# An attention and feed-forward kernel on one core: a new order of the same operations, and row factors of unit 0 spread by two TensorE products

## Chip, cores and metric

One core of a Trainium2 chip runs the whole program in one launch. The metric is the device time of that launch in microseconds (us); a kernel's time is the median of its runs. Engines are named as the profile names them: PE is TensorE's matrix multiply and PEld its weight load, DVE is VectorE, ACT ScalarE, POOL GpSimd, SP SyncE, which issues the DMAs.

## What is computed

Attention in which a query sees only the keys of its own hash bucket (six sign bits of a projection), for 4 batches of 8 heads with 768 tokens of 64 values, and behind it a feed-forward layer with the Mish function for the 3072 tokens. The two weight matrices arrive as 64-bit floats.

```python
q_bits = (np.einsum('bhsd,dk->bhsk', q, proj) > 0)        # k_bits likewise, 6 bits
mask = q_bucket[:, :, :, None] == k_bucket[:, :, None, :]
scores = np.where(mask, scale * np.matmul(q, k.transpose(0, 1, 3, 2)), -1e9)
attn = np.exp(scores - np.max(scores, axis=-1, keepdims=True))
attn = attn / (np.sum(attn, axis=-1, keepdims=True) + 1e-09)
x = np.matmul(attn, v)                                    # to 3072 x 512
h = x @ w_in                                              # 512 x 2048
out = (h * np.tanh(np.log1p(np.exp(h)))) @ w_out          # 2048 x 512
```

## The kernel before

The work is cut into 12 units (4 batches, 3 pairs of 128-row chunks). A unit has 8 **scores** n (4 pairs of heads, 2 chunks), 96 in all, and behind them 8 groups of the feed-forward layer, which run about three blocks of four scores later. For each score:

- `S` on PE (line 879): eight products of queries (`QT`) and keys (`KT`) into `ps_s`, 128 x 1536 in PSUM, two heads beside each other. From unit 1 on there is one `ps_s`, so the next score's products wait until this score's exponentials have read it.
- `max` on DVE (line 885) over `ps_s`, then `scl` (lines 891 to 897), two to four tiny instructions on DVE or POOL that make the scale and bias of the exponential. They come as two instructions on 128x2 or, with the same result, four on 128x1.
- `exp` on ACT (line 910), once per head, from `ps_s` into one of three buffers `pb`, with row sums. Where ACT ran Mish last, a table load stands before it.
- `sums` (lines 923, 926) and `rv`, the reciprocal (line 939, DVE): the row factors.
- `hi` for each head (lines 373, 375, 376 for POOL, ACT, DVE): `pb` times the row factor, as 16-bit floats, into `hl`; then `lo`, what `hi` left over. On DVE `lo` is one instruction with two SBUF inputs (line 391); on POOL it is two (line 397 scales `pb` in place, line 398 subtracts `hl`). Only after `lo` is that `pb` buffer free.
- a DMA transposes `hl` into `PT` (line 408), and `V` on PE (line 997) multiplies `PT` by the values.

Keys, queries, values and weights are split into a high and a low 16-bit part in the same manner (`k_lo`, `q_lo`, `v_lo`, `w_lo`, all through lines 391 or 397/398); the first 24 scores run beside the conversion of the weights from 64-bit floats (lines 540 to 565). The feed-forward group is `H` (lines 1053 to 1055) into `ps_acc`, Mish on ACT (line 1071), `g_hi` and `g_lo` (lines 373 to 376, 391) into `ffb`, and `O` (lines 1104 to 1106).

Unit 0 differs: its exponentials are transposed on PE as 32-bit floats, and the row factors are applied after `V`. `rvw` (line 935, DVE) writes the reciprocals spread over 128 columns into a piece of `X`; `rvb` (line 943, PE) multiplies that by a unit matrix (`ffb` holds it) into `ps_g`; `rvc` copies it out.

Nothing is scheduled while the kernel runs. `Plan.op` records every operation with its alternatives, `alts` (which engine does it, and in which form), and `ORDER`, a string of 2753 numbers, gives the sequence: the number names the operation, a letter b, c or d behind it the second, third or fourth alternative. Each engine runs its instructions in that sequence.

Of the kernel before, what the change touches and what calls it, by code (L numbers as in the profile page):

```python
# [18 lines left out]
P = 128  # L19
# [68 lines left out]
1 88 0 5 2 3 4 14 22 23 24 25b 38b 13 40 6 37 7 8 9 10 11b 63 73 39c 65 78 18 19 20 21 53c 55b 26c 41 42 27 74 75 76  # L88
15 67 43 72 54c 66 44 307 12 45 46 83 47 48 49 104 28b 29 79 62 168 30b 31 77b 89 91b 32 34 213 214 215 90c 50 51 64
33 80 84 52 35 81 82 92 105 85 86 87 107 113 216b 114c 115c 116b 106 36 108 109 56 57 58 59 60 110 68 217 71 17 93 94  # L90
95 96 97 99 98 16 100 61 117 169 170 171 172 173c 175 176 256 372 153c 112 101 102 103b 257 258 111 129 130 132 133
134 152 154b 155 156 70 135 136 137 138 139 118 119 120 121 122 147 148 131 123b 124b 125 157 158 205 206b 140b 69 162
163b 164 144 149 150 151 182c 177 159 160 161 178 308 309 310b 145 146b 373 374 183 126 185 186 187 141 188 189 190
142 458 200 211 218b 191 192 459 197 198 201 202 203 174c 460 461b 193b 378 379 204 219c 194 128 143b 195 184 196 127
230 222 223 224 180 179 181 199b 225 243 212 462 380 165 166 226 227 207b 208 254 228 229 240 241 464 167 244 245b 210
209 220 221 255 231b 232 233 234 465 466 311 242 268 248c 249b 236b 237 259 246 269 270 250 251 235 286 247 273c 274
238 265 266 293c 239 262c 263 305 312b 306 252 267 287 272 271 279 381 253 294b 280 283 284 275b 276 278 299 288 289
277 295c 296 300b 298 297 301 264 285 281 292 291 290 313b 314 315b 370 282 371 326c 327 317b 318 321 322 323 324 432
434 302 303 304 332 333 334 328c 329 331 330 325 352 353 433 457 344d 456 316 319b 345 347b 350b 260c 335 336 354 435
# [12 lines left out]
679 699 680b 681 720 746 718 683b 725c 726 721c 672 754 673 727 612 722 768 799 690 691 692c 694 695 767 747 751 755
693c 696 697 752b 753 613 748b 749 806 757b 758b 728 729 730 731 759 760 761 763 856 807 808 809 769 684 682b 733 734
775 735 736 762 770 771 772 764 798 685 774 800 737 686 687 860 773 801 857 873 688 756 689 738 765b 855 739 740 741
861 877 790d 791 793c 796 797 802 803 792c 794 864 862b 863 742 743 744 874 804 805 821 858 859 895 766 812 813 814c
816b 795 810b 815b 875c 822 776 777 778 779 780 811b 910 820 881 823 781c 783 818 876 878 879 824 825 847d 848 849 880
745 851 931 782b 868 869 882 961 700 894 817 850b 865 870 784 785 786 909 788 826 827 828 829 830 831 872 883 871 896
911 945 819 852 853b 854 932 832b 886 887 889 787 888c 962 897 917 898b 890b 900 842 899 789 912 833 835 891 834b 836
892 893 933 934 964 901b 902 903b 913 914b 915 905 906 843 844 845 1147 916 937c 965 968 969 938 918 904b 907b 939c
941 942 908 948 949 837 838 977 978 981 846 963 970c 950 951 940b 943b 944 979c 980 966c 967 1046 952 972 840 953 954  # L120
956b 959b 982 983 971 1047 839 955c 919 935b 920 921 922b 924b 1050 1051 946 957 985 958 960 973 1148 925 866 974 976
975 988 1064 989 991c 990 992b 998 999 1000b 994 1020 1001 1060 1021 1022 841 923c 1002 1003c 1004 1005b 984 1061 997
993 1006c 1007b 1102 926 927 1054 884 885b 1014 867 1149 1015 995 1009 1010 1008 996 1011 1048b 1049 1065 1013 928
# [115 lines left out]
def lsh_attention_mish_ffn(  # L239
# [10 lines left out]
    nc = tc.nc  # L250
    B, H, S, D = q.shape
# [17 lines left out]
    op = plan.op  # L269
# [14 lines left out]
    unit = ffb.rearrange("p n e -> p (n e)")[:, 3584:3712]  # L284
    UNIT = ("ff", 3584, 3712)
# [134 lines left out]
    def dve(name, ns, fn, reads, writes, frees=None):  # L420
        return op(name, [("DVE", ns, fn)], reads, writes, frees=frees)
# [838 lines left out]
```

## Time and profile before

| what | us |
|---|---|
| median of 3 runs | 964.82 (963.01 to 965.0) |
| the profiled execution's own time | 964.74 |
| its span, first to last instruction | 963.0 |
| PE, DVE, ACT, POOL busy | 831.7, 733.8, 574.2, 513.3 |
| mean granted TensorE clock | 0.957 of full |

Outside the span lie 1.74 us. A busy time is the union of an engine's instructions and includes what an instruction spends blocked after it has started.

### The profile page before, as it was taken

How to read it: one execution, taken by the hardware profiler on the slowest of the kernel's cores; microseconds unless marked ns; L12 is line 12 of the kernel's file. 1: busy time of each engine (PE TensorE's matmuls, PEld its weight loads, DVE VectorE, ACT ScalarE, POOL GpSimd, SP SyncE). 2: the span in 40 equal slices, each digit the busy share in tenths (PEclk: the TensorE clock that was granted, in tenths of full speed). 3: DMA queues.
4: the chain of work that ended last, by engine and by line, in shares of the span. 5: the costliest groups of instructions: out<-in, count | busy, mean ns of one | idle time of the engine just before them, and what ended most of it. 6: DMA issues, size and time to landing. Idle time of an engine off the chain costs nothing. (4 is left out here: it accounts for less than half of the span.)

```text
span 963.0 us, 16924 instructions
## 1 busy us (share of the span) xinstructions
PE 831.7 (86%) x6492; PEld 556.4 (58%) x6492; DVE 733.8 (76%) x1211; ACT 574.2 (60%) x898; POOL 513.3 (53%) x424
## 2 busy tenths in 40 slices
PE   4778777768989899979999889889889789999998
PEld 3555454444658557547566466556557447576474
DVE  5899998998788767778888867768786877676611
ACT  4555546665757557557777537547548647667421
POOL 6457788675376554352456635363764643625410
PEclk9799998887999999999999999989999989999999
DMA  8856755736897768589977757578977556664700
GB/s 279 158 178 200 203 123 118 138 86 136 168 186 137 146 124 154 109 176 167 228 147 147 146 94 163 102 152 161 174 148 144 103 106 116 129 115 84 150 16 22
DMA packets 400305, 135.60 MB, mean 141 GB/s; under 512 B 370528, under 2 KB 391008, under 8 KB 400224
## 3 DMA queue, kind: packets, MB, share of 16 engines
q1 hardware_dynamic: 400224, 134.52, 68.5%
q8 instruction: 51, 0.84, 0.4%
q14 instruction: 30, 0.25, 0.1%
HBM read 35.65 MB, written 6.29 MB: 44 GB/s over the span
## 5 line engine op out<-in xcount | busy, mean ns | idle before, releaser
L910 ACT ACTIVATE pb<-ps_s,svb 128x768 f32<-128x768 f32 x192 | 188.8, 987 | 143.9 <-DVE svb L897 85.7
L879 PE MATMUL ps_s<-KT,QT 128*128 128x512 f16 (+1 forms) x768 | 153.1, 346 | 54.0 <-ACT pb L910 52.5
L1053 PE MATMUL ps_acc<-X,wi 128*128 128x256 f16 x704 | 195.0, 277 | 2.6 <-ACT ffb L1071 2.4
L1054 PE MATMUL ps_acc<-X,wi 128*128 128x256 f16 x704 | 194.8, 277 | 1.0 <-DVE X L1024 1.0
L1055 PE MATMUL ps_acc<-X,wi 128*128 128x256 f16 x704 | 194.6, 276 | 0.0
L885 DVE TENSOR_REDUCE svb<-ps_s 128x2 f32<-128x1536 f32 x96 | 167.8, 1748 | 19.9 <-PE ps_s L879 19.6
L1106 PE MATMUL ps_o<-wo,ffb 128*128 128x512 f16 x352 | 134.5, 382 | 10.7 <-DVE ffb L391 10.7
L879 PEld LDWEIGHTS <-QT 128*128 128x128 f16 x768 | 76.7, 102 | 115.9 <-issue 74.9
L398 POOL TENSOR_TENSOR hl<-pb,hl 128x768 f16<-128x768 f32 x80 | 139.1, 1739 | 6.7
L373 POOL TENSOR_SCALAR hl<-pb,svb 128x768 f16<-128x768 f32 x65 | 75.2, 1158 | 122.6 <-DVE svb L939 68.3
L1104 PE MATMUL ps_o<-wo,ffb 128*128 128x512 f16 x352 | 134.9, 383 | 0.0
L391 DVE SCALAR_TENSOR_TENSOR hl<-pb,svb,hl 128x768 f16<-128x768 f32 x96 | 124.1, 1297 | 14.1 <-ACT hl L375 6.7
L1105 PE MATMUL ps_o<-wo,ffb 128*128 128x512 f16 x352 | 134.4, 382 | 0.0
L397 POOL TENSOR_SCALAR pb<-pb,svb 128x768 f32<-128x768 f32 x80 | 89.5, 1118 | 79.1 <-ACT hl L375 34.0
L997 PE MATMUL ps_t<-PT,VT 128*64 128x256 f16 x1584 | 98.2, 277 | 8.4 <-DMA PT<-hl 8.4
L997 PEld LDWEIGHTS <-VT 128*64 128x64 f16 x1584 | 84.9, 111 | 25.7 <-issue 14.6
L910 ACT ACT_TABLE_LOAD x49 | 62.9, 1283 | 61.7 <-DVE svb L897 48.6
L391 DVE SCALAR_TENSOR_TENSOR ffb<-ffb,smalls 128x512 f16<-128x512 f32 x88 | 78.9, 906 | 23.6 <-ACT ffb L375 13.2
L1071 ACT ACTIVATE ffb<-ps_acc,smalls 128x512 f32<-128x512 f32 x88 | 59.3, 686 | 52.8 <-PE ps_acc L1055 41.8
L1054 PEld LDWEIGHTS <-wi 128*128 128x128 f16 x704 | 69.9, 99 | 16.8 <-issue 4.9
L1053 PEld LDWEIGHTS <-wi 128*128 128x128 f16 x704 | 69.9, 99 | 13.5 <-issue 2.8
L1055 PEld LDWEIGHTS <-wi 128*128 128x128 f16 x704 | 70.0, 99 | 10.4 <-issue 1.2
(221 smaller groups left out, 1266.5 us busy)
## 6 DMA issues: line engine op xcount, KB each, us to landing
out_dram<-ffb SPq DMA_DIRECT2D x24, 256.0 KB, 2.8
stg<-in_q_dram SPq DMA_DIRECT2D x10, 512.0 KB, 4.7
stg<-in_k_dram SPq DMA_DIRECT2D x12, 384.0 KB, 4.0
stg<-in_v_dram SPq DMA_DIRECT2D x12, 384.0 KB, 4.1
wo<-in_moe_w_out_dram SPq DMA_DIRECT2D x7, 512.0 KB, 4.4
stg<-in_moe_w_out_dram SPq DMA_DIRECT2D x7, 512.0 KB, 3.8
wi<-in_moe_w_in_dram SPq DMA_DIRECT2D x6, 512.0 KB, 4.6
stg<-in_moe_w_in_dram SPq DMA_DIRECT2D x6, 512.0 KB, 4.3
```

Source lines behind the costliest of these rows:

```text
L391: return [("DVE", 215 + 1.035 * n, port(lambda: nc.vector.scalar_tensor_tensor(out=dst, in0=src, scalar=sc, in1=hi, op0=ALU.mult, op1=ALU. ...
L398: nc.gpsimd.tensor_tensor(out=dst, in0=src, in1=hi, op=ALU.subtract)
L879: nc.tensor.matmul(sc[:, hh * S + c0 * P:hh * S + c1 * P], QTb[:, u % 2, sl, qi], KTb[:, j, sl, hh * NCH + c0:hh * NCH + c1].rearrange("p ...
L885: op("max", [("DVE", 1790, lambda: nc.vector.tensor_reduce(out=sv[:, 0], in_=sc.rearrange("p (h e) -> p h e", h=2), axis=AX.X, op=ALU.max, ...
L910: EXP[n, hh] = op("exp", [("ACT", 1075, lambda hh=hh, t=t: nc.scalar.activation(pb[:, t], sc[:, hh * S:(hh + 1) * S], AF.Exp, bias=sv[:, 2 ...
L997: nc.tensor.matmul(pv[hh * D:(hh + 1) * D, 0:256], vt[:, w, hh * NCH + c], pt[:, hh, a * NCH + c].rearrange("p s t -> p (s t)"), start=(x ...
L1053: nc.tensor.matmul(o, wh, X[:, 0, c], start=(c == 0), stop=False)
L1054: nc.tensor.matmul(o, wh, X[:, 1, c], start=False, stop=False)
L1055: nc.tensor.matmul(o, wl, X[:, 0, c], start=False, stop=(c == NCC - 1))
L1104: nc.tensor.matmul(PS[f"o{s}"], gh, hi[:, e], start=first, stop=False)
L1105: nc.tensor.matmul(PS[f"o{s}"], gh, lo[:, e], start=False, stop=False)
L1106: nc.tensor.matmul(PS[f"o{s}"], gl, hi[:, e], start=False, stop=last)
```

## The change

Every operation stays, with its number; 2753 stand in both orders. What changes is the whole of `ORDER` (its first line stands here for all) and, in `att_back`, the row factors of unit 0.

```diff
 ORDER = """
-1 88 0 5 2 3 4 14 22 23 24 25b 38b 13 40 6 37 7 8 9 10 11b 63 73 39c 65 78 18 19 20 21 53c 55b 26c 41 42 27 74 75 76
+14 88 0 152 22 1 2 3 4 23 24 25 63 73 38c 40 7 6 8 9 5 13 74 10 11 12 41 18 19 20 21 75 26c 28 42 43 76 53b 55 67 105
...
-        if u == 0:
-            rw = 768 + n % 2 * P
-            rt = x_w[:, 1, rw:rw + P]
-            dve("rvw", 230, lambda: nc.vector.reciprocal(
-                rt.rearrange("p (h d) -> p h d", h=2), sv[:, 5].rearrange("p (h o) -> p h o", o=1).broadcast_to([P, 2, D])),
-                [f"{x}.rs"], [("X1", rw, rw + P)])
-        else:
-            dve("rv", 165, lambda: nc.vector.reciprocal(sv[:, 4], sv[:, 5]), [f"{x}.rs"], [f"{x}.rv"])
+        dve("rv", 165, lambda: nc.vector.reciprocal(sv[:, 4], sv[:, 5]), [f"{x}.rs"], [f"{x}.rv"])
...
-            op("rvb", [("PE", 250, lambda: nc.tensor.matmul(ps_g[:, 256 + s * P:256 + (s + 1) * P], rt, unit, start=True,
-                                                            stop=True))], [("X1", rw, rw + P), UNIT], [f"gr{2 + s}"])
+            def spread():
+                for hh in range(2):
+                    nc.tensor.matmul(ps_g[hh * D:(hh + 1) * D, 256 + s * P:256 + (s + 1) * P],
+                                     sv[:, 4, hh:hh + 1].broadcast_to([P, D]), unit, start=True, stop=True)
+            op("rvb", [("PE", 250, spread)], [f"{x}.rv", UNIT], [f"gr{2 + s}"])
```

Where the alternatives went, counted in the two orders (before to after):

| operation | DVE | ACT | POOL |
|---|---|---|---|
| `lo` (176) | 96 to 164 | | 80 to 12 |
| `hi` (176) | 66 to 73 | 45 to 78 | 65 to 25 |
| `g_hi` (88) | 34 to 41 | 24 to 39 | 30 to 8 |
| `k_lo`, `q_lo`, `v_lo`, `w_lo` (61) | 39 to 55 | | 22 to 6 |
| `w_u`, `w_sign`, `w_low` (54) | 15 to 19 | 7 to 14 | 29 to 18 |
| `scl` (96) | 87 to 90 | | 9 to 6 |

By stretches, from one score to another: the wide POOL instructions (512 columns or more) between score 8 and score 24 go from 81 to 32, between 24 and 56 from 114 to 63, between 56 and 88 from 112 to none, and behind 88 from 29 to none. `lo` on DVE in the same stretches: 18 to 28, 35 to 56, 31 to 62, 12 to 18. ACT's table loads go from 100 to 96.

POOL in unit 1 (between scores 8 and 16) before: `wo`, `wi` and `stg` are weights, `VT` values.

```order
L373 TENSOR_SCALAR hl<-pb,svb 128x768
L397 TENSOR_SCALAR pb<-pb,svb 128x768
L398 TENSOR_TENSOR hl<-pb,hl 128x768
L373 TENSOR_SCALAR VT<-wo,smalls 128x768
L397 TENSOR_SCALAR wo<-wo,smalls 128x768
L398 TENSOR_TENSOR VT<-wo,VT 128x768
L549 TENSOR_SCALAR wo<-stg 128x1024
L553 TENSOR_SCALAR wo<-stg 128x1024
L549 TENSOR_SCALAR wi<-wi 128x1024
```

POOL in the same unit after:

```order
L548 TENSOR_SCALAR wo<-wo 128x512
L372 TENSOR_SCALAR wo<-wo 128x512
L372 TENSOR_SCALAR stg<-stg 128x512
L548 TENSOR_SCALAR wo<-stg 128x512
L446 TENSOR_SCALAR smalls<-hw 128x1
L446 TENSOR_SCALAR smalls<-ho 128x1
L372 TENSOR_SCALAR wo<-wo,smalls 128x1024
L372 TENSOR_SCALAR wi<-wi,smalls 128x1024 x2
```

The pairs of lines 397 and 398 are gone from this piece of POOL's queue; what is left has one tensor input.

DVE from the maximum of score 69 to that of score 70, before (line numbers of `max`, `scl`, hash bits, `g_lo`, `rv`, `hi`, `lo`):

```order
L885 TENSOR_REDUCE svb<-ps_s 128x2
L891 TENSOR_SCALAR svb<-svb,smalls 128x2
L897 TENSOR_TENSOR svb<-svb 128x2
L717 TENSOR_REDUCE hsum<-ps_t 128x72
L721 TENSOR_SCALAR tok_65<-hsum 128x12x6 x2
L391 SCALAR_TENSOR_TENSOR ffb<-ffb,smalls 128x512
L939 RECIPROCAL svb<-svb 128x2
L376 TENSOR_SCALAR hl<-pb,svb 128x768
L391 SCALAR_TENSOR_TENSOR hl<-pb,svb,hl 128x768
L885 TENSOR_REDUCE svb<-ps_s 128x2
```

DVE between the same two maxima after (each line number is one or more lower):

```order
L884 TENSOR_REDUCE svb<-ps_s 128x2
L890 TENSOR_SCALAR svb<-svb,smalls 128x2
L896 TENSOR_TENSOR svb<-svb 128x2
L390 SCALAR_TENSOR_TENSOR ffb<-ffb,smalls 128x512
L390 SCALAR_TENSOR_TENSOR hl<-pb,svb,hl 128x768
L390 SCALAR_TENSOR_TENSOR VT<-stg,smalls,VT 128x768
L931 RECIPROCAL svb<-svb 128x2
L850 TENSOR_SCALAR smalls<-smalls 128x1
L375 TENSOR_SCALAR hl<-pb,svb 128x768
L390 SCALAR_TENSOR_TENSOR hl<-pb,svb,hl 128x768
L884 TENSOR_REDUCE svb<-ps_s 128x2
```

A second `lo` and a `v_lo` have come between the two maxima, and the hash bits have moved elsewhere.

DVE around unit 0's first row factors, before (`ps_s_90` is a second score buffer of unit 0):

```order
L926 TENSOR_SCALAR svb<-svb 128x2
L935 RECIPROCAL X<-svb 128x128
L391 SCALAR_TENSOR_TENSOR wo<-wo,smalls 128x12x64
L885 TENSOR_REDUCE svb<-ps_s_90 128x2
L891 TENSOR_SCALAR svb<-svb,smalls 128x2
L897 TENSOR_TENSOR svb<-svb 128x2
```

DVE at the same place after:

```order
L925 TENSOR_SCALAR svb<-svb 128x1 x2
L461 TENSOR_SCALAR smalls<-ps_t 128x1
L384 COPY wo<-wo 128x12x64
L390 SCALAR_TENSOR_TENSOR wo<-wo,smalls 128x12x64
L931 RECIPROCAL svb<-svb 128x2
```

The reciprocal of 128x128 has become one of 128x2; on PE each `rvb` is now two products of 64 columns of weights where it was one of 128.

## Rows read from the trace of the kernel before

**Rows 1.** The page, busy time of each engine with its share of the span.

```profile
PE 831.7 (86%) x6492; PEld 556.4 (58%) x6492; DVE 733.8 (76%) x1211; ACT 574.2 (60%) x898; POOL 513.3 (53%) x424
```

**Rows 2.** Six stretches: length, busy per engine (instructions), granted clock, DMA share, GB/s.

```profile
0.00:20.10 20.10, 8.39 (x95) 7.12 (x96) 10.07 (x38) 10.36 (x19) 12.73 (x22) 1.00 0.95 294
20.10:74.90 54.80, 41.32 (x328) 29.64 (x327) 48.95 (x92) 31.98 (x54) 27.15 (x23) 0.88 0.66 167
74.90:272.70 197.80, 155.38 (x967) 99.75 (x966) 182.03 (x245) 116.54 (x178) 138.71 (x100) 0.90 0.66 147
272.70:551.60 278.90, 255.78 (x2151) 172.51 (x2150) 219.23 (x387) 184.54 (x295) 146.67 (x122) 0.99 0.82 155
551.60:843.60 292.00, 259.00 (x2083) 172.01 (x2082) 219.42 (x361) 175.92 (x273) 153.72 (x128) 0.96 0.70 134
843.60:963.00 119.40, 111.79 (x875) 75.36 (x873) 54.13 (x94) 54.86 (x82) 34.32 (x31) 1.00 0.37 76
```

**Rows 3.** Line 879 (S) alone in two of these stretches: eight products are one score.

```profile
272.70:551.60 278.90, 49.20 (x256) 25.18 (x256) 0.99 0.82 155
551.60:843.60 292.00, 51.71 (x256) 25.71 (x256) 0.96 0.70 134
```

**Rows 4.** Waits of the whole span: who for whom, total us, times, longest.

```profile
ACT pb L910 <- DVE svb L897: 85.7, 27, 6.3
PE ps_s L879 <- ACT pb L910: 52.5, 38, 3.8
ACT L910 <- DVE svb L897: 48.6, 21, 7.3
PE ps_t L997 <- DMA PT<-hl: 8.4, 5, 3.9
```

**Rows 5.** Groups by line and shape, whole span: busy us, mean ns | idle before.

```profile
L398 POOL TENSOR_TENSOR hl<-pb,hl 128x768 f16<-128x768 f32 x80 | 139.1, 1739 | 6.7
L391 DVE SCALAR_TENSOR_TENSOR hl<-pb,svb,hl 128x768 f16<-128x768 f32 x96 | 124.1, 1297 | 14.1 <-ACT hl L375 6.7 <-POOL hl L373 6.0
L397 POOL TENSOR_SCALAR pb<-pb,svb 128x768 f32<-128x768 f32 x80 | 89.5, 1118 | 79.1 <-ACT hl L375 34.0 <-DVE hl L376 28.0 <-DVE smalls L851 11.9
L891 DVE TENSOR_SCALAR svb<-svb,smalls 128x2 f32<-128x2 f32 x61 | 37.5, 614 | 1.8
L897 DVE TENSOR_TENSOR svb<-svb 128x2 f32<-128x2 f32 x61 | 22.0, 360 | 2.1
```

**Rows 6.** One line each, whole span: shortest/median/longest ns, first and last start.

```profile
L391 DVE SCALAR_TENSOR_TENSOR hl<-pb,svb,hl x96: 999/1019/3058, 104.0 to 907.7; 128x768 f16<-128x768 f32 x96
L376 DVE TENSOR_SCALAR hl<-pb,svb x66: 605/620/2073, 102.7 to 902.8; 128x768 f16<-128x768 f32 x66
L891 DVE TENSOR_SCALAR svb<-svb,smalls x113: 99/219/1645, 25.3 to 902.4; 128x2 f32<-128x2 f32 x61, 128x1 f32<-128x1 f32 x52
L897 DVE TENSOR_TENSOR svb<-svb x61: 160/160/1560, 25.4 to 871.4; 128x2 f32<-128x2 f32 x61
```

**Rows 7.** DVE's groups in 74.9 to 272.7 (scores 8 to 24), as in Rows 5.

```profile
L885 DVE TENSOR_REDUCE svb<-ps_s 128x2 f32<-128x1536 f32 x16 | 27.9, 1745 | 0.2
L391 DVE SCALAR_TENSOR_TENSOR hl<-pb,svb,hl 128x768 f16<-128x768 f32 x17 | 27.9, 1642 | 1.9 <-ACT hl L375 1.1 <-POOL hl L373 0.5
L891 DVE TENSOR_SCALAR svb<-svb,smalls 128x2 f32<-128x2 f32 x11 | 7.0, 636 | 0.3
```

**Rows 8.** One collision in time on POOL, DVE and ACT: start us, length us.

```profile
711.88 1.64 POOL L398 TENSOR_TENSOR hl<-pb,hl 128x768 f16<-128x768 f32 x1
...
712.52 1.82 DVE L391 SCALAR_TENSOR_TENSOR hl<-pb,svb,hl 128x768 f16<-128x768 f32 x1
...
714.38 0.99 ACT L910 ACTIVATE pb<-ps_s,svb 128x768 f32<-128x768 f32 x1 [1.71 <-DVE hl L391]
```

**Rows 9.** Unit 0's row factors, lines 935 and 943, as in Rows 6.

```profile
L935 DVE RECIPROCAL X<-svb x8: 939/950/953, 30.8 to 78.3; 128x128 f32<-128x128 f32 x8
L943 PE MATMUL ps_g<-ffb,X x16: 272/275/377, 35.5 to 79.6; 128*128 128x128 f32 x16
```

More of the change, by code (lines that the diff above doesn't have):

```diff
@@ L198 @@
[L198 to L200 removed]
+14 88 0 152 22 1 2 3 4 23 24 25 63 73 38c 40 7 6 8 9 5 13 74 10 11 12 41 18 19 20 21 75 26c 28 42 43 76 53b 55 67 105
+29 15 83 44 45 37 39b 46 47 65 78 30 71 213 31 54 48 49 27c 50 16 32 34 214 70 215 104 33 35 79 36 84 56 77b 89 80 81
@@ new lines @@
+379 380 209 225 210 226 227 250b 286 223 251 253 254 310 180 220 212 195 184 196b 230 231b 255 229 228 240 241 232c
+233 107 224 243 244 245 242 268 269 273b 311b 305 236d 246 247 265 465 375 237 461b 266 181 238 234 274b 270 271 262
+376 272 283 263 284 275c 276 267 279c 285 259b 287 221 239 466 235 260 370 293c 292 294 295b 252 280 299 467b 277 288
+289 290 291 300 301b 278 281 296 264 282b 371 313b 314 306 218b 315b 321 322 326b 316 432 297 327 381 357 462b 298
+323c 317 261 318 325 302 319 324 344d 345 312 304 433 346c 348 347 434 435 332b 352 353 354 355 328 329 350 303 333
@@ new lines @@
+415 420 421b 422c 423 564 501 519c 520 446 478 455 521c 523 480 543 544 522 528 481 364 511 512 565 622 636 529 530
+598 567 545b 546c 547 600 531 365 366 368 581 623 513b 514 515 367 525 582 583 532 533 534 666 584 524 599 548 536c
+549 601 482 447 585 369 550 551 535 552b 539 602 603 586 624 526 553 587 642 540 559 625 537 604 605b 626 627 628 538
+588 589 667 590b 591 560 561b 629 592 568 563 562 571 572 574c 655 656 569 607 674 657 577b 593 594 643 644 645 646
+595c 630 631 632 608 573 698 633 575 576 634c 675 647b 648 635 609 610 596 597 614b 615 701 606b 649 637 702 703 578
@@ new lines @@
+1519 1520 1578 1486 1564 1565 1498 1529 1464b 1566 1596 1421 1530 1531 1522 1532 1567b 1544 1579 1521c 1465 1597 1467b
+1468 1469 1466b 1523 1533 1534 1535c 1537 1545 1600 1598 1536 1599 1628 1568 1546 1594 1629 1549 1524 1525 1601 1613
+1470 1538 1471 1548 1539 1547 1569c 1550 1580 1602c 1603 1570 1571c 1573 1574 1609 1595 1614 1610 1611b 1581 1572b
+1582c 1584 1644 1472 1551 1643 1473 1477b 1583 1552 1553b 1585d 1612 1540 1678 1905 1679 1604 1554c 1556 1734 1575
+1557 1586 1588b 1651 1555b 1587 1605 1606b 1607 1692 1589 1608 1620c 1680 1735 1686 1682 1683 1615c 1616 1693 1630
@@ new lines @@
+2642b 2643 2644c 2646 2645 2677 2651 2652 2653 2654 2655 2650 2684 2676 2686 2688 2685 2687 2689 2647 2648 2649 2681
+2656 2657 2659 2658c 2660 2662 2678 2679b 2680 2682 2696 2683 2661 2663 2690 2691 2692 2693 2694 2699 2700 2701b 2582
+2697b 2695 2698 2703 2704 2705b 2702 2716 2715 2706 2718 2717 2707 2708 2711 2709b 2710 2719 2720 2712 2713c 2714 2721
+2722 2723 2724 2727 2728 2725c 2726 2739 2740 2729c 2730 2742 2741 2731 2732 2733c 2734 2735 2736 2737c 2744 2743 2738
+2745 2747b 2746b 2748 2749 2750b 2751b 2752
```

202 lines of the change are left out of this document (90 added, 112 removed).

## Prediction

> **What bounds the kernel now.** I read the page's busy line first. PE is busy 831.7 of 963.0 us and DVE 733.8 [rows 1], and a mean over the span does not tell which of them limits what, so the second view is a table of six stretches cut at scores 0, 8, 24, 56 and 88 [rows 2]. It shows two regimes. From score 8 to 24 (74.9 to 272.7) DVE is busy 182.0 of 197.8 us, 92%, and PE only 155.4: while the weights are converted, DVE sets the pace. From score 24 to 88 PE is busy 255.8 of 278.9 and 259.0 of 292.0 us, DVE 79% and 75%. There are 32 scores in each of these two stretches (256 products of S, eight a score [rows 3]), so a score takes 8.7 and 9.1 us.
>
> The waits say what holds PE there [rows 4]: its longest is S for the exponential of the score before (52.5 us, 38 times), since one `ps_s` serves both, and the exponential and its table load wait for `scl` on DVE (85.7 and 48.6). The loop S, max, scl, exp, S turns with PE's work. DMA is no rival for PE: 8.4 us of waits.
>
> The third reading is why DVE is slow. The `lo` of 128x768 has a median of 1019 ns and a mean of 1297, with a longest of 3058; the two instructions of `scl` have medians of 219 and 160 ns and means of 614 and 360 [rows 5, 6]. An instruction of 128x2 cannot need 1645 ns by itself. [rows 8] shows what happens: POOL subtracts from 711.88 to 713.52; DVE's `lo` starts at 712.52 and ends at 714.34, 0.82 us after POOL's end, as if it had stood still until then. The exponential on ACT, which needs that `pb` buffer, starts at 714.38. The maximum, which reads PSUM, shows nothing of the kind: 1745 ns amid the busiest POOL [rows 7].
>
> So POOL's work is paid twice, once on POOL and again on DVE. The change takes most of it away and gives DVE and ACT the work. The sum weighs these two.
>
> **The change, part by part.** I go by stretches, against the profiled execution (964.74 us, 0.08 below the median of the runs; 1.74 lie outside its span).
>
> *Before score 8 (74.9 us).* Eight reciprocals of 950 ns [rows 9] become eight of 128x2. That form isn't in these rows, but DVE's smallest instructions take 160 to 219 ns [rows 6]: 8 x 0.75 = 6 us less on DVE, which is busy 48.95 of 54.8 us there [rows 2]. PE gets eight more pairs of passes of at most 0.28 us each, some 4 us, and is busy 41.3 of 54.8; they are behind a reciprocal that comes earlier, so I cost them at nothing, at +4 if each is waited for. ACT gets more copies. I take -3, between -6 and +4.
>
> *Scores 8 to 24 (197.8 us).* Added to DVE: ten `lo` at 1.02 us are 10.2, three `v_lo` of the same shape 3.1, three `k_lo` and `q_lo` 3.3; the rest (fewer `hi` and weight parts, more sign bits) about cancels: +16 us. Removed: collisions. Seventeen `lo` lose 17 x (1642 - 1019) = 10.6 us and eleven of `scl` 11 x (636 - 219) = 4.6, so 15.2 of their 34.9 us [rows 6, 7]. The maxima (27.9) lose nothing. Of the remaining 119 us nothing may be lost, or the same 44%, 52 us; some of it is tiny or from PSUM, so I take a little over half, 30: 45 in all, between 15 and 67. POOL's wide instructions fall from 81 to 32, so 60% goes: -27, between -9 and -40. Net 16 - 27 = **-11 us**, between +7 and -24, and nearly all of it shows, since DVE leaves only 15.8 us idle.
>
> *Scores 24 to 56 (278.9 us) and 56 to 88 (292.0).* Here the loop counts. The 61 `scl` in the 128x2 form lose 61 x ((614 - 219) + (360 - 160)) = 36 us in the whole span [rows 5, 6], 0.60 each; 61 of 96 scores have it, so 32 scores carry 20 of them, 12 us. From 24 to 56 POOL keeps 63 of 114 wide instructions, so 45% of that goes, 5.5; from 56 to 88 POOL is empty and all 12 go. Then `pb`: a `lo` on POOL takes 1118 + 1739 ns against 1019 on DVE [rows 5, 6], so 20 and 31 halves free their buffer 1.8 us earlier; the exponential waits for that seldom, and I take 2 us for each stretch (0 to 10). Against it stands the new load. DVE gets 21 and 31 `lo` more; with the other moves about +22 and +48 us. From 56 to 88 its collisions go: by the three groups of [rows 5, 6] 26.7 + 36 = 63 us in the span, less some 18 before score 24, leave 45 for 690 us, so about 19 in this stretch. DVE then does 219 + 48 - 19 = 248 us, 88% of some 281. A maximum finds DVE busy more often. I cost this at +1 and +3 us (up to 10 and 25 if every fourth or so of the new `lo` stands in front of a waiting maximum). Net **-6.5** (between -15 and +5) and **-11** (between -26 and +13).
>
> *Behind score 88 (119.4 us).* PE is busy 111.8; the end is O and its store. **-1** (between -4 and +2).
>
> Sum: -3 - 11 - 6.5 - 11 - 1 = -32.5, so 964.74 - 32.5 = **932 us**. ACT is not late in it: `hi` and `g_hi` bring it 48 instructions, none with more columns than the exponential of 0.99 us [rows 8], on top of 574 busy [rows 1]. The transposes behind `lo` move with it in SP's queue; their number stays, so the DMA share of 0.82 between scores 24 and 56 [rows 2] rises only as the time falls, and I cost them at nothing; the cover is the three blocks between `lo` and `V`, and without it PE's 8.4 us of waits [rows 4] would be what grows. The clock is left out: it was 0.88 and 0.90 of full before score 24 [rows 2], the lower of its levels (1.2 GHz against 2.4) in part of the time, around PE's idle pieces. Fewer of these give some back, and a PE that waits for DVE there gains little by it.
>
> **A rule that speaks against it.** DVE is at 92% from score 8 to 24, and the change puts 16 us more on it. The Trainium skill, Perfetto Trace Analysis, Optimizing Scalar/DVE Operations, says that where DVE is saturated, moving work to ScalarE or even GpSimd may make sense, and adds that the two share an SBUF port, so that moving between these two might not help. By its first half the stretch would grow by the 16 us, to 213.8, and the whole to 981; [rows 8] is what its second half describes. It is the second rival.
>
> **Rivals.** (1) *More than forecast.* Once no `scl` and no `lo` is stretched, the other gaps close too: PE's own busy time is 255.8 + 259.0 of 570.9 us [rows 2]. If half of the 56 idle us goes and the first 24 scores give the -24 and -6 of their bounds: 964.74 - 28 - 30 - 4 = 903, and less with clock given back. For it: short waits and long ones come from the same loop. Against: the loop S, max, scl, exp itself stays.
>
> (2) *Slower: DVE's queue takes the place of the collision.* Price: the added 16 + 22 + 48 = 86 us of DVE against the measured part of the collisions alone, 63 x 0.85 = 53, is +33 if all of it lands on the path, 998; with half of it 981. Place: scores 56 to 88, where 48 us more on DVE are 1.5 us a score, before each maximum. It decides once over 0.6 us of these (what `scl` gives back), 40%, fall between a score's products and its maximum. For it: DVE at 88% in order. Against: in the piece between scores 69 and 70 what is new stands behind `scl`, ahead of the next maximum, where S is still to come.
>
> (3) *No change: the wait moves.* `scl` ends earlier, and the exponential waits for its table load, Mish or a `pb` buffer instead: only the first 24 scores give anything, 955 to 965. ACT's table load waits for `scl` as the exponential does (48.6 us [rows 4]), so it is not hidden today; that speaks against.
>
> That the order doesn't do what it says is ruled out by its rows: 80 `lo` on POOL become 12.
>
> **How the numbers follow.** A measurement tells about 0.2% from no change, so "same" is 962.9 to 966.8. Chances: as forecast, 903 to 950, 0.60; rival 1, below 903, 0.12; rival 3, 950 to 967, 0.13, two thirds of it below 962.9; rival 2, above 967, 0.15. Faster 0.60 + 0.12 + 0.08 = 0.80, same 0.05, slower 0.15. The bounds of the terms add up to 964.74 - 76 = 889 and 964.74 + 31 = 996; not all reach their ends together. From 894 to 972 leaves out some 0.08 below and 0.11 above.
>
> **What would show it.** Right: means of `lo` and `scl` on DVE near their medians of 1.02, 0.22 and 0.16 us, to the nanosecond behind score 56; scores 8 to 24 at some 187 us with DVE still above 85% busy; 8.5 to 8.7 us a score from 24 to 88; PE's wait for exp clearly below 52.5 us. Wrong: DVE above 90% behind score 56 with the wait before S unchanged (rival 2); means at their medians and the score's period still near 9 us (rival 3); `lo` still at 1.3 us with POOL nearly idle, which would mean that something else than POOL stretched it.

## The result, and the profile after

The changed kernel takes 856.87 us (median of 4 runs, 853.46 to 857.61), the kernel before beside it 963.91. The ratio is 0.8882, 95% interval 0.8856 to 0.8909: 107 us, or 11%, faster. The forecast was 932 us and its range ended at 894. The direction was right and the size was not. Of the runs told of below, one (1042.01 us at a granted clock of 0.757, of the kernel with its last 12 `lo` moved) was in a slow state and is left out of that kernel's ratio.

The page's busy line of the kernel after, which answers to [rows 1]:

```profile
PE 802.6 (94%) x6508; PEld 550.4 (64%) x6508; DVE 703.5 (82%) x1313; ACT 622.2 (73%) x955; POOL 158.9 (19%) x167
```

The same six stretches as [rows 2], cut at scores 0, 8, 24, 56 and 88 of the kernel after:

```profile
0.00:15.40 15.40, 7.41 (x80) 6.67 (x81) 8.05 (x36) 9.45 (x16) 8.66 (x15) 1.00 0.90 290
15.40:71.00 55.60, 46.22 (x366) 33.39 (x364) 46.02 (x93) 39.14 (x61) 24.91 (x26) 0.91 0.80 218
71.00:228.50 157.50, 139.15 (x933) 92.67 (x931) 150.19 (x260) 130.31 (x191) 47.98 (x46) 0.98 0.79 172
228.50:490.50 262.00, 254.54 (x2169) 173.87 (x2169) 215.44 (x404) 189.79 (x294) 77.31 (x82) 1.00 0.90 169
490.50:740.10 249.60, 244.29 (x2098) 168.67 (x2097) 221.94 (x419) 197.06 (x309) 0.00 (x0) 1.00 0.81 155
740.10:855.10 115.00, 110.95 (x875) 75.08 (x873) 61.85 (x105) 56.51 (x85) 0.00 (x0) 1.00 0.39 79
```

| scores | before, us | after, us | difference | forecast |
|---|---|---|---|---|
| to 8 | 74.9 | 71.0 | -3.9 | -3 |
| 8 to 24 | 197.8 | 157.5 | -40.3 | -11 |
| 24 to 56 | 278.9 | 262.0 | -16.9 | -6.5 |
| 56 to 88 | 292.0 | 249.6 | -42.4 | -11 |
| behind 88 | 119.4 | 115.0 | -4.4 | -1 |

Two things stand out. DVE got dozens of wide instructions more (1313 records for 1211) and is busy 30 us less. And PE is busy 94% of the span, from score 56 to 88 98%: it now hardly waits. Its longest wait, 52.5 us in [rows 4], is:

```profile
PE ps_s L878 <- ACT pb L909: 11.2, 12, 3.3
```

The instructions of [rows 6], one line each over the whole span (shortest, median, longest ns), have kept their medians and lost most of what lay above them:

```profile
L390 DVE SCALAR_TENSOR_TENSOR hl<-pb,svb,hl x164: 997/1017/2271, 81.3 to 799.8; 128x768 f16<-128x768 f32 x164
L890 DVE TENSOR_SCALAR svb<-svb,smalls x112: 198/228/1486, 20.1 to 795.2; 128x2 f32<-128x2 f32 x68, 128x1 f32<-128x1 f32 x44
L896 DVE TENSOR_TENSOR svb<-svb x68: 160/160/968, 20.4 to 795.4; 128x2 f32<-128x2 f32 x68
```

### The profile page after: what moved, and what is told of

It reads as the page before. It is cut to its first block, busy times and chain, and to the rows that moved or that the text cites. A ratio compares the mean times of both kernels' runs of the same rounds, so it can differ in the third digit from the quotient of the medians.

```text
span 855.1 us, 16728 instructions
## 1 busy us (share of the span) xinstructions
PE 802.6 (94%) x6508; PEld 550.4 (64%) x6508; DVE 703.5 (82%) x1313; ACT 622.2 (73%) x955; POOL 158.9 (19%) x167
## 5 line engine op out<-in xcount | busy, mean ns | idle before, releaser
L1048 PE MATMUL ps_acc<-X,wi 128*128 128x256 f16 x704 | 191.9, 273 | 2.4 <-POOL wi L381 1.3
L1050 PE MATMUL ps_acc<-X,wi 128*128 128x256 f16 x704 | 191.9, 273 | 0.0
L1049 PE MATMUL ps_acc<-X,wi 128*128 128x256 f16 x704 | 191.8, 272 | 0.0
L390 DVE SCALAR_TENSOR_TENSOR hl<-pb,svb,hl 128x768 f16<-128x768 f32 x164 | 168.7, 1037 | 13.0 <-ACT hl L374 6.2
L878 PE MATMUL ps_s<-KT,QT 128*128 128x512 f16 (+1 forms) x768 | 143.4, 330 | 12.5 <-ACT pb L909 11.2
L878 PEld LDWEIGHTS <-QT 128*128 128x128 f16 x768 | 73.4, 98 | 64.3 <-issue 21.9
L992 PE MATMUL ps_t<-PT,VT 128*64 128x256 f16 x1584 | 95.1, 274 | 6.0 <-DMA PT<-hl 5.0
L374 ACT ACTIVATE hl<-pb,svb 128x768 f16<-128x768 f32 x78 | 71.9, 930 | 32.9 <-DMA PT<-hl 9.4
L390 DVE SCALAR_TENSOR_TENSOR ffb<-ffb,smalls 128x512 f16<-128x512 f32 x88 | 66.6, 763 | 19.4 <-ACT ffb L374 16.1
L1049 PEld LDWEIGHTS <-wi 128*128 128x128 f16 x704 | 68.8, 98 | 13.8 <-issue 2.2
L1048 PEld LDWEIGHTS <-wi 128*128 128x128 f16 x704 | 68.8, 98 | 13.4 <-POOL wi L381 1.6
L909 ACT ACT_TABLE_LOAD x47 | 60.3, 1283 | 19.4 <-DVE svb L896 15.1
L1050 PEld LDWEIGHTS <-wi 128*128 128x128 f16 x704 | 68.8, 98 | 8.2 <-issue 0.2
L1101 PEld LDWEIGHTS <-ffb 128*128 128x128 f16 x352 | 34.4, 98 | 41.8 <-DVE ffb L390 0.4
```

The costliest lines, as they stand in the source:

```text
L390: return [("DVE", 215 + 1.035 * n, port(lambda: nc.vector.scalar_tensor_tensor(out=dst, in0=src, scalar=sc, in1=hi, op0=ALU.mult, op1=ALU. ...
L878: nc.tensor.matmul(sc[:, hh * S + c0 * P:hh * S + c1 * P], QTb[:, u % 2, sl, qi], KTb[:, j, sl, hh * NCH + c0:hh * NCH + c1].rearrange("p ...
L909: EXP[n, hh] = op("exp", [("ACT", 1075, lambda hh=hh, t=t: nc.scalar.activation(pb[:, t], sc[:, hh * S:(hh + 1) * S], AF.Exp, bias=sv[:, 2 ...
L992: nc.tensor.matmul(pv[hh * D:(hh + 1) * D, 0:256], vt[:, w, hh * NCH + c], pt[:, hh, a * NCH + c].rearrange("p s t -> p (s t)"), start=(x ...
L1048: nc.tensor.matmul(o, wh, X[:, 0, c], start=(c == 0), stop=False)
L1049: nc.tensor.matmul(o, wh, X[:, 1, c], start=False, stop=False)
```

## Experiments

What was to be settled: is it the collisions between POOL and DVE that cost 107 us, or is the new sequence simply better, with the engines secondary? An entry of `ORDER` has a number (place in the sequence) and a letter (engine and form), so the two can be separated.

### The two products of unit 0 alone

The kernel before, its order untouched, with the second hunk of the diff.

```diff
-            dve("rvw", 230, lambda: nc.vector.reciprocal(
...
+        dve("rv", 165, lambda: nc.vector.reciprocal(sv[:, 4], sv[:, 5]), [f"{x}.rs"], [f"{x}.rv"])
```

> The kernel before with unit 0's row factors spread by two TensorE products, nothing else. Both theories: eight reciprocals shrink from 0.95 to about 0.17 us, 6 us less VectorE work before score 8; 958 to 964 us, that is 0 to 6 us faster. 964 or more would mean that this part is worth nothing by itself.

962.34 us, ratio 0.9996 (0.9979 to 1.0013). No difference can be told, although DVE does what was expected; its busy time on the page falls from 733.8 by 6.8 us:

```profile
PE 833.7 (87%) x6508; PEld 557.1 (58%) x6508; DVE 727.0 (76%) x1211; ACT 573.9 (60%) x898; POOL 509.9 (53%) x424
```

So this part, at least in the old order, is not where the 107 us are. Everything else is `ORDER`.

### The engines alone, and the sequence alone

First the sequence of the kernel before with the letters of the changed one (509 entries differ):

```diff
-22 23 24 25b 38b 13 40 6 37 7 8 9 10 11b 63
+22 23 24 25 38c 13 40 6 37 7 8 9 10 11 63
```

> The kernel before with its own sequence of operations, but each operation on the engine and in the form that the changed kernel gives it (12 lo on GpSimd instead of 80); unit 0's row factors as before. Theory 'collisions' (GpSimd's work stretches VectorE's instructions, and taking it off GpSimd is the gain): lo near 1.04 us on VectorE, and most of the 107 us comes with the engines alone, 870 to 900 us. Theory 'sequence' (the new order lets each instruction stand where its inputs are ready, and the engines matter little): VectorE has 96 us more work in an order that was not made for it, 935 to 980 us.

1049.51 us, ratio 1.090 (1.0868 to 1.0931): 9% **slower** than the kernel before, outside what either theory expected. The busy line of its page:

```profile
PE 850.4 (81%) x6492; PEld 564.8 (54%) x6492; DVE 717.3 (68%) x1313; ACT 627.4 (60%) x959; POOL 165.2 (16%) x167
```

Of the same run, the groups by shape (line, engine, operation, tiles, shapes and count | busy us, mean ns of one | idle us just before them and what ended it):

```profile
L390 DVE SCALAR_TENSOR_TENSOR hl<-pb,svb,hl 128x768 f16<-128x768 f32 x164 | 170.1, 1047 | 55.9 <-ACT hl L374 44.3 <-POOL hl L372 9.9
```

Of the same run, PE's wait for the exponential in the list of waits (us in all, count, the longest):

```profile
PE ps_s L878 <- ACT pb L909: 82.3, 48, 5.7
```

Most collisions are gone, 1047 ns a `lo` and DVE down to 717.3 us, and the time is worse. What DVE does now in front of each `lo` is wait, 55.9 us, mostly for `hi` on ACT: the entries stand where another engine once had them, each engine works strictly in order, and behind a `lo` that waits stands the next score's maximum.

Then the opposite, the new sequence with the old letters:

```diff
-4 23 24 25 63 73 38c 40 7 6 8 9 5 13 74
+4 23 24 25b 63 73 38b 40 7 6 8 9 5 13 74
```

> The changed kernel with its own sequence of operations, but each operation on the engine and in the form that the kernel before gave it (80 lo on GpSimd); unit 0's row factors in the new way. 'Collisions': lo on VectorE back at about 1.3 us mean, 940 to 990 us although VectorE has 96 us less to do than in the changed kernel. 'Sequence': 860 to 900 us.

1032.83 us, ratio 1.0719 (1.0673 to 1.0765). Also slower, by more than the collisions had been expected to do, and outside both ranges. The busy line of its page:

```profile
PE 846.7 (83%) x6508; PEld 564.4 (55%) x6508; DVE 709.2 (69%) x1211; ACT 567.3 (55%) x894; POOL 501.4 (49%) x424
```

Of the same run, the groups by shape (line, engine, operation, tiles, shapes and count | busy us, mean ns of one | idle us just before them and what ended it):

```profile
L391 DVE SCALAR_TENSOR_TENSOR hl<-pb,svb,hl 128x768 f16<-128x768 f32 x96 | 116.9, 1221 | 29.8 <-POOL hl L373 15.7 <-ACT hl L375 12.8
```

Each half of the change loses 70 to 86 us and both together gain 107. A sequence is worth something only with the engines it was laid out for. That does not yet say why the new pair is better than the old one, which beats both mixtures too. The next runs leave each fitting pair as it is and change only the collisions.

### POOL filled again in the changed kernel

From score 56 to 88 POOL is empty in the changed kernel. This run gives it work whose results nobody needs, at the pace of the scores; `jo` is 832 columns of zeros, and `...` marks what is left out:

```diff
...
+    jo = tok1[:, :, 12:64]
...
+    for o, fn in plan.ordered():
         fn()
+        if o.name != "rv":
+            continue
+        rv = svb[:, n % NSV, 4, 0:1]
+        if 56 <= n < 88:
+            nc.gpsimd.tensor_scalar(out=jo, in0=jk, scalar1=rv, scalar2=0.0, op0=ALU.mult, op1=ALU.mult)
+            nc.gpsimd.tensor_scalar(out=jo, in0=jk, scalar1=rv, scalar2=0.0, op0=ALU.mult, op1=ALU.mult)
+            nc.gpsimd.tensor_tensor(out=jo, in0=jk, in1=jk, op=ALU.subtract)
+        n += 1
```

> The changed kernel with work on GpSimd that nobody needs from score 56 to 88, where its GpSimd is empty: for each score two one-input instructions of 832 columns and one with two SBUF inputs, started by the score's reciprocal, as hi and lo were; they write zeros over zeros. VectorE's work, the order and the buffers stay. 'Collisions': lo and scl stretch again, and scores 56 to 88 (249.6 us) go to 265 to 290: 872 to 900 us in all. 'Sequence', or that GpSimd's lo mattered because it held a pb buffer for 2.9 us: nothing waits for this work, 855 to 862 us.

896.26 us, ratio 0.9305 (0.9278 to 0.9332): 39 us slower than the changed kernel. The busy line of its page:

```profile
PE 810.2 (91%) x6508; PEld 550.6 (62%) x6508; DVE 745.0 (83%) x1313; ACT 622.7 (70%) x955; POOL 293.4 (33%) x263
```

Of the same run, scores 56 to 88 in the table of stretches:

```profile
489.70:779.20 289.50, 253.05 (x2097) 170.24 (x2096) 262.95 (x419) 197.88 (x309) 130.88 (x95) 0.98 0.71 135
```

The stretch takes 289.5 us where it took 249.6, as long as before the change (292.0 [rows 2]). DVE has the same 419 instructions and is busy 262.95 us instead of 221.94: 41.0 us of stretched instructions, 39.9 us of time. PE's wait is back as well:

```profile
PE ps_s L878 <- ACT pb L909: 35.4, 28, 3.9
```

`lo` within that stretch (as in [rows 5]), in the kernel before, in the changed kernel and in this run:

```profile
L391 DVE SCALAR_TENSOR_TENSOR hl<-pb,svb,hl 128x768 f16<-128x768 f32 x33 | 41.5, 1266 | 4.5 <-ACT hl L375 3.5 <-POOL hl L373 0.4
...
L390 DVE SCALAR_TENSOR_TENSOR hl<-pb,svb,hl 128x768 f16<-128x768 f32 x64 | 64.7, 1016 | 4.3 <-ACT hl L374 2.9 <-issue 0.3
...
L390 DVE SCALAR_TENSOR_TENSOR hl<-pb,svb,hl 128x768 f16<-128x768 f32 x64 | 80.7, 1266 | 4.4 <-ACT hl L374 3.3
```

So a busy POOL costs this much by itself, with the order, the engines, the buffers and DVE's work untouched. That POOL's `lo` mattered because it kept a `pb` buffer is not needed to explain it. Two things come with the filling and are in its price. SP, which issues the DMAs, had to wait for it four times:

```profile
SPq L407 <- POOL tok L1237: 11.7, 4, 3.6
```

Little of this reached DVE: in the stretch it is idle for 26.6 us here and 27.7 without the filling. And the granted clock is 0.98 instead of 1.00, with PE busy 253.05 us instead of 244.29 for the same products; how much of the 39.9 us that is, the run does not separate.

### What kind of work on POOL

Two more fillings of the same place: four one-input instructions for each score, and five memsets behind one tiny instruction. Of each, one instruction stands here:

```diff
+            nc.gpsimd.tensor_scalar(out=jo, in0=jk, scalar1=rv, scalar2=0.0, op0=ALU.mult, op1=ALU.mult)
...
+            nc.gpsimd.memset(jo, 0.0)
```

> The same place, four one-input instructions of 832 columns for each score on GpSimd and none with two inputs. If it is GpSimd's two-input instructions that stretch VectorE: 855 to 865 us. If every instruction that reads SBUF does: 885 to 905 us, as e4 (896).

892.09 us, ratio 0.9258 (0.9222 to 0.9293), the same as with two inputs within their intervals:

```profile
PE 810.3 (91%) x6508; PEld 551.5 (62%) x6508; DVE 742.3 (83%) x1313; ACT 624.3 (70%) x955; POOL 311.1 (35%) x295
```

> The changed kernel with work on GpSimd that nobody needs from score 56 to 88, as in e4, but work that reads next to nothing: for each score one tiny instruction that the score's row sums start and five memsets of 832 columns (zeros over zeros), about as long in all. If GpSimd stretches VectorE because both read SBUF: lo (two SBUF inputs) stays near 1.03 us and the kernel within 855 to 868 us; if a busy GpSimd does it whatever it runs: 885 to 900 us as e4.

873.42 us, ratio 0.9066 (0.9037 to 0.9095), between the two cases that were expected. The busy line of its page:

```profile
PE 803.1 (92%) x6508; PEld 548.4 (63%) x6508; DVE 719.4 (82%) x1313; ACT 622.8 (71%) x955; POOL 301.6 (35%) x359
```

Of the same run, the groups by shape (line, engine, operation, tiles, shapes and count | busy us, mean ns of one | idle us just before them and what ended it):

```profile
L390 DVE SCALAR_TENSOR_TENSOR hl<-pb,svb,hl 128x768 f16<-128x768 f32 x164 | 167.3, 1028 | 12.7 <-ACT hl L374 6.2 <-POOL hl L372 4.4
...
L375 DVE TENSOR_SCALAR hl<-pb,svb 128x768 f16<-128x768 f32 x73 | 50.9, 697 | 11.1 <-DMA PT<-hl 9.7
L890 DVE TENSOR_SCALAR svb<-svb,smalls 128x2 f32<-128x2 f32 x68 | 28.3, 416 | 2.0
...
L896 DVE TENSOR_TENSOR svb<-svb 128x2 f32<-128x2 f32 x68 | 12.9, 190 | 2.3
```

The same rows of the changed kernel without filling:

```profile
L390 DVE SCALAR_TENSOR_TENSOR hl<-pb,svb,hl 128x768 f16<-128x768 f32 x164 | 168.7, 1037 | 13.0 <-ACT hl L374 6.2 <-POOL hl L372 4.3 <-issue 0.3
...
L375 DVE TENSOR_SCALAR hl<-pb,svb 128x768 f16<-128x768 f32 x73 | 45.8, 627 | 3.5 <-DMA PT<-hl 1.8 <-DVE svb L931 0.3
L890 DVE TENSOR_SCALAR svb<-svb,smalls 128x2 f32<-128x2 f32 x68 | 21.6, 318 | 2.0
...
L896 DVE TENSOR_TENSOR svb<-svb 128x2 f32<-128x2 f32 x68 | 13.0, 191 | 2.3
```

Memsets leave alone what has two SBUF inputs, `lo` (1028 against 1037 ns) and the second instruction of `scl` (190 against 191), and stretch the one-input `hi` (697 against 627) and the first instruction of `scl` (416 against 318). The Trainium skill, SBUF — State Buffer, Who interferes with whom, has this pattern: the two engines lock a shared pair of ports for a whole instruction; a VectorE instruction with two SBUF inputs meets only GpSimd work that reads, one in a two-port mode meets any. The rows agree. For this kernel it means that "two SBUF inputs" on POOL is not the point: 152.2 us of one-input work on POOL cost 37.6 us of span, 134.5 us with two-input work among it 39.1, and 142.7 us of memsets 18.4. These 18.4 us are not stretch alone. SP waited for the memsets and the tiny instructions ahead of them (13.5 us in five waits), and DVE's `hi` waited 9.7 us for the transposes (`DMA PT<-hl`) instead of 1.8.

### The collisions taken out of the kernel before

Order, engines and waits of the kernel before; POOL's wide work becomes memsets of about the same length, with a tiny instruction at its ends that reads `pb` and `hl`, so this kernel leaves out the results of that work. The edit of `lo`; `hi` has one of the same kind:

```diff
-            nc.gpsimd.tensor_scalar(out=src, in0=src, scalar1=sc, scalar2=1.0, op0=ALU.mult, op1=ALU.mult)
-            nc.gpsimd.tensor_tensor(out=dst, in0=src, in1=hi, op=ALU.subtract)
+            nc.gpsimd.tensor_scalar(out=two(src), in0=two(src), scalar1=sc, scalar2=1.0, op0=ALU.mult, op1=ALU.mult)
+            for _ in range(3):
+                nc.gpsimd.memset(dst, 0.0)
+            nc.gpsimd.tensor_tensor(out=two(dst), in0=two(src), in1=two(hi), op=ALU.subtract)
```

> The kernel before, in its own order and on its own engines, but GpSimd's wide work on pb, ffb, keys, queries, values and split weights (hi, lo, g_hi and the like) is replaced by memsets of about the same length with a tiny instruction that reads the first two columns, so that what waits for it still waits; the results are left out with that, 16-bit and 64-bit conversion of the weights stays. 'Collisions': the order before was as good as the new one and was only stretched by them; lo on VectorE near 1.03 us and 870 to 915 us. 'Fit' (the gain of the change is an order that suits its engines, and the collisions cost little in the old one): 940 to 965 us.

897.14 us, ratio 0.932 (0.9297 to 0.9344): 65 us of the 107, without moving one operation, and within the range of 'collisions'. The busy line of its page:

```profile
PE 809.4 (90%) x6492; PEld 550.0 (61%) x6492; DVE 653.9 (73%) x1211; ACT 573.5 (64%) x898; POOL 507.2 (57%) x847
```

Of the same run, the groups by shape (line, engine, operation, tiles, shapes and count | busy us, mean ns of one | idle us just before them and what ended it):

```profile
L400 DVE SCALAR_TENSOR_TENSOR hl<-pb,svb,hl 128x768 f16<-128x768 f32 x96 | 102.2, 1069 | 9.9 <-ACT hl L384 5.4 <-POOL hl L380 3.0
```

Of the same run, PE's wait for the exponential in the list of waits (us in all, count, the longest):

```profile
PE ps_s L890 <- ACT pb L921: 28.0, 27, 3.7
```

The old order was not a bad one: its `lo` took 1.30 us on the mean, and with 1.07 the same order is 65 us faster. Not all is settled by this run, since memsets still stretch `hi` and `scl`, and POOL's conversion of the weights stays. But four runs now have the same DVE work as their neighbour and differ only in how much of it is stretched, so the price can be read from busy time and span on the pages:

| run, against | DVE busy, us | span, us | us of span per us of DVE |
|---|---|---|---|
| filling with two- and one-input work, after | +41.5 | +39.1 | 0.94 |
| one-input filling, after | +38.8 | +37.6 | 0.97 |
| memsets, after | +15.9 | +18.4 | 1.16 |
| memsets for POOL's work, before | -79.9 | -68.1 | 0.85 |

By the medians of the runs in place of the two spans the last column reads 0.95, 0.91, 1.04 and 0.82; the memset row also holds the waits for DMA named above.

**A microsecond by which POOL stretches DVE cost about a microsecond of time** in these two orders with their own engines, with DVE busy 73% to 83% of the span. Between the kernel before and the one after, DVE's busy time falls by 30.3 us while it is given some 86 to 90 us of work more (16 + 22 + 48 by the prediction's count, a few behind score 88): some 118 us of stretch are gone. At 0.85 to 0.97 that is 100 to 114 us (137 at the 1.16 of the memset row), and 107.9 us of span were gained. So collisions can account for the whole gain. What the added DVE work cost in the new order does not come out of this: from nothing to some 30 us would fit. This is arithmetic over runs, with the prediction's count of the added work in it; no run took out every collision.

### How much the fit is worth

The engines of before behind score 56 only, in the new sequence (191 entries differ):

```diff
-1777 1687 1688 1738 1674 1689b 1700 1701 1702 1690 1691 1703c 1704 1779 1781
+1777 1687 1688 1738b 1674 1689 1700 1701 1702 1690 1691 1703c 1704 1779 1781
```

> The changed kernel, but every operation that stands behind the products of score 56 goes to the engine that the kernel before gave it (37 lo, 32 hi and 21 g_hi back on GpSimd), in the sequence of the changed kernel. If collisions alone make the difference, VectorE's smaller load makes up for some: 880 to 897 us, not above e4. If the engines' order also has to fit: 905 to 940 us.

905.93 us, ratio 0.9417 (0.9384 to 0.945), at the lower edge of "fit". It is 10 us above the filled kernel, although DVE has 67 records less to do than there, 1246 for 1313:

```profile
PE 807.5 (89%) x6508; PEld 547.4 (61%) x6508; DVE 684.9 (76%) x1246; ACT 595.0 (66%) x914; POOL 343.5 (38%) x328
```

Its last two stretches, cut at scores 56 and 88:

```profile
486.80:779.90 293.10, 255.12 (x2098) 171.50 (x2097) 210.56 (x364) 174.31 (x273) 151.57 (x130) 0.97 0.69 133
779.90:902.90 123.00, 112.53 (x874) 74.95 (x873) 54.77 (x93) 52.23 (x80) 33.05 (x31) 0.99 0.35 73
```

Most of the 10 us lie behind score 88 (123.0 us, against 115.0 in the filled kernel, whose POOL is empty there). From 56 to 88 it takes 293.1 us, against 289.5 filled, although DVE is busy 52 us less: what DVE is spared buys nothing here. Some of it goes into waits (DVE waits 21.5 us for exponentials and 19.4 us for row sums on ACT). The kernel before takes 292.0 in this stretch [rows 2], so with the old engines the two sequences are equally long there.

The sequence-only kernel with memsets for POOL's wide work (the edit of the kernel before, above):

> As e2 (the changed kernel's sequence with the engines of the kernel before, 1032.8 us), with GpSimd's wide work replaced by memsets as in e7; the results of that work are left out. e2 had about 127 us of stretched VectorE instructions; if they cost 0.9 us each here too and some 60 of them go, 970 to 985 us, and what lies between that and 857 is the misfit of sequence and engines. If misfit is all of e2's loss: 1020 to 1035. If collisions are: below 920.

992.65 us, ratio 1.0314 (1.0255 to 1.0373), against 1032.83 with collisions: 40 us less, where 50 to 60 were expected, and outside all three ranges.

```profile
PE 844.1 (85%) x6508; PEld 564.6 (57%) x6508; DVE 645.3 (65%) x1211; ACT 567.1 (57%) x894; POOL 503.6 (51%) x847
```

DVE is busy 63.9 us less than in the sequence-only run, so only 0.45 us of span per us, counted between the two spans (1022.4 and 993.5), or 0.63 by the medians (the profiled execution of the sequence-only run was its fastest). That part of a stretch is hidden where engines wait for each other anyway is the likely reading; no run shows it. The kernel before with the same engines and the same memsets takes 897.14 us, so some 95 us of this run belong to the misfit of sequence and engines.

At last, the rest of POOL's work moved off in the changed kernel: 12 `lo` to DVE, and in a second run also 25 `hi` and 8 `g_hi` to ACT.

```diff
-607 674 657 577b 593 594 643 644 645 646 595c 630 631 632 608
+607 674 657 577 593 594 643 644 645 646 595c 630 631 632 608
```

> The changed kernel with its last 12 lo taken from GpSimd to VectorE, in the same sequence. If every collision that goes is a gain (about 0.9 us for each us by which VectorE is stretched, as in e4 to e7): a few us of the 9 that VectorE still loses between scores 24 and 56, 848 to 855 us. If VectorE's order must fit its work: 12 more us of VectorE in places not made for them, 857 to 872 us.

> The changed kernel with the last 12 lo on VectorE and the last 25 hi and 8 g_hi on ScalarE instead of GpSimd, in the same sequence. Collisions alone: 845 to 853 us. Fit: 865 to 890 us.

864.02 us (ratio 0.8978, 0.8914 to 0.9042) and 890.86 us (0.9242, 0.919 to 0.9295); the changed kernel has 0.8882. Neither is better; the first lies in the range of 'fit', the second just above it. The busy line of the first run's page:

```profile
PE 797.8 (93%) x6508; PEld 545.7 (64%) x6508; DVE 710.0 (83%) x1325; ACT 622.2 (72%) x955; POOL 127.1 (15%) x143
```

And of the second run's:

```profile
PE 813.1 (91%) x6508; PEld 551.7 (62%) x6508; DVE 708.0 (80%) x1325; ACT 647.2 (73%) x988; POOL 98.5 (11%) x110
```

33 instructions moved from POOL to ACT without a new sequence cost 27 us, though DVE is busy 2 us less. No run beat the changed kernel; a planner that lays the sequence out anew around an emptier POOL was not tried.

## Why the prediction was wrong in size

**What bounds the kernel** was read rightly: DVE from score 8 to 24, the loop S, max, scl, exp behind it, and in both POOL's work paid for twice [rows 8]. The three fillings and the memsets in the kernel before show that reading at work. Most signs named for it came: from score 56 to 88 `lo` takes 1016 ns on the mean, PE's wait for the exponential is 11.2 us, DVE is busy 95% from score 8 to 24. A score took 8.2 and 7.8 us, less than the 8.5 to 8.7 given.

**Before score 8**: -3, measured -3.9. Near, but it proves little: the filled kernels and the one with the engines of before behind score 56, which have the changed kernel's start, reach score 8 at 65.8 to 70.5 us, the changed kernel itself at 71.0. The shorter reciprocals by themselves are worth nothing that can be measured in the whole time.

**Scores 8 to 24**: -11, measured -40.3. The 45 us of collisions were sized well. The step that failed is "POOL's wide instructions fall from 81 to 32, so 60% goes". DVE went from 182.0 to 150.2 us with 16 more to do, so 48 are gone, all that I had counted: the share of POOL's instructions that goes is no measure of the share of collisions that goes. `lo` takes 1081 ns on the mean in this stretch now, instead of 1642 [rows 7], beside the 32 wide instructions that are left. Whether that is for their place in the order or for their kind, no run separates. What the stretch lost beyond DVE, 40.3 against 31.8, is idle DVE that closed up.

**Scores 24 to 88**: -6.5 and -11, measured -16.9 and -42.4. Most of the miss lies here and in scores 8 to 24. Two errors in one term, the collisions. The size: I scaled three groups by length to 19 us of collisions from 56 to 88; DVE's 219.4 + 48 - 221.9 = 45 went, and from 24 to 56 219.2 + 22 - 215.4 = 26. The value: I let only `scl`'s share reach the path, 5.5 and 12 us, since `scl` is a link of the loop; the stretch of `lo`, `hi` and `g_lo` entered DVE's load (the 248 us) and was put at nothing on the path, without a reason. The filled kernel shows 39.9 us of time for 41.0 us of stretch, with DVE idle as long as without the filling. The likely way: DVE works in order, so a `lo` that takes 0.8 us longer puts the next maximum back by as much, and idle DVE time in another place doesn't absorb it.

**The new load**: +1 and +3 us for DVE's queue, with the second rival behind it. In the changed kernel DVE is at 89% from score 56 to 88 and PE at 98%, so little of it can be on the path there. The first half of what the Trainium skill's Perfetto Trace Analysis, Optimizing Scalar/DVE Operations, says, which I priced at +16 us for scores 8 to 24, is not what happened (40.3 us less, with that work added); its warning about the shared port fits the rows. Yet the second rival's mechanism is real: with the old sequence the same load on the same engines gave 1049.51 us. I had no way to tell a fitting sequence from a misfit by counts of what moved where, and the trace of before cannot show it.

**The clock** was left out. It was 0.88 and 0.90 of full before score 24 [rows 2] and is 0.91 and 0.98; behind that it is 1.00 instead of 0.96 to 1.00. PE's busy time fell from 831.7 to 802.6 us with 16 more records, a part of which is this. In the filled kernel, where only POOL's work was added, the clock falls to 0.98 again, so there it follows the collisions; how much of the 29 us it is, no run separates.

**The rivals**: the first, more than forecast, is what happened, at a chance of 0.12 and a price of 903 that was still 46 us short, because it closed half of PE's gaps and gave nothing for the clock; 56 idle us between scores 24 and 88 became 13 (511.6 less 254.5 and 244.3). It also held scores 8 to 24 at -24, where 40.3 us went. The third, that the wait moves, did not happen.

**The bounds** hold two small slips: the terms given for scores 56 to 88 reach -22, not -26, and the lower bounds as stated add up to -75, not -76. Neither bears on the miss.

## What to carry to other kernels

Where VectorE and GpSimd both work from SBUF, compare each VectorE group's mean with its median, and look in the timeline whether GpSimd was busy beside the long ones: the excess may be GpSimd's work billed a second time. In this kernel's fitting orders it was worth 0.85 to 1.16 us of time for each us, also where VectorE was not the bound and the instruction was no link of the loop. Sum it over all groups; where the median is stretched too, as from score 8 to 24, the excess over it is too small. Engines and sequence have to be changed together: each of them alone made this kernel 7 to 9% slower where both made it 11% faster, so an experiment that moves work between engines in a fixed order says little about the move.

## What the runs showed of the hardware

A VectorE instruction on 128x2 values can be held up like a wide one, and the same work on 128x1 was not: in the run with the filled GpSimd the first instruction of `scl` took 436 ns on the mean in the one form (318 in the changed kernel) and 209 in the other, as in the changed kernel.

```profile
L890 DVE TENSOR_SCALAR svb<-svb,smalls 128x2 f32<-128x2 f32 x68 | 29.6, 436 | 2.0
...
L890 DVE TENSOR_SCALAR svb<-svb,smalls 128x1 f32<-128x1 f32 x44 | 7.3, 209 | 0.7
```

Size alone does not decide it: the reciprocal of 128x2 takes 163 ns on the mean in both runs. A GpSimd that only writes, in memsets, stretched the one-input `hi` (697 against 627 ns) and not the two-input `lo` (1028 against 1037). A column of 128x1, repeated over 64 columns as weights, makes no pass of PE slower: the passes of unit 0's products have a median of 273 ns, against 275 for 128 full columns in [rows 9], though there are two of them for each one before.
